# Reordering the last four experts of a fused attention, MLP and mixture-of-experts kernel, and the side work that is spread over two of its sections

## The chip, the cores and the metric

The kernel runs on one core of a Trainium2 chip. The metric is the device time of one execution, in microseconds (us). Several executions were timed; the median is the figure of merit, and one more execution was recorded by the hardware profiler. TensorE (PE) does the matmuls, VectorE (DVE) and ScalarE (ACT) the elementwise work, GpSimd (POOL) issues the indirect DMAs, and SyncE (SP) issues all other DMAs, each engine in its own program order.

## The reference

Three stages follow each other. The change touches only the last one, a mixture of eight experts on 2304 tokens:

```python
def _moe2_ref(x, w_skip, w_gate, w1, w2):
    do_compute = x @ w_skip > 0
    out = x.copy()
    xc = x[do_compute]
    logits = xc @ w_gate
    e_idx = np.argmax(logits, axis=1)
    ...
    for e in range(E):
        mask = e_idx == e
        h = np.maximum(xc[mask] @ w1[e], 0.0)
        y[mask] = gate_w[mask, None] * (h @ w2[e])
    out[do_compute] = xc + y
    return out
```

A token goes to one expert, or to none. `w1[e]` is 512 x 1024 and `w2[e]` is 1024 x 512, in float32. So an expert has eight pieces of 128 x 1024 numbers (512 KB each): pieces 0 to 3 are `w1`, pieces 4 to 7 are `w2`. The program calls the two groups of four the halves 0 and 1 of an expert: "2-1" is `w2` of expert 2, "3-0" is `w1` of expert 3.

## The kernel before

**How an expert is prepared.** All experts but one are multiplied in float16, each weight as the sum of a high and a low part. A half is loaded by four DMAs (`load_w`, in order on SP; "l" or "m" in the table below), its sums of squares or maxima are taken ("s", `stat_w`: ACT with `Square`, or DVE), a power of two is worked out from them ("c", `scale_w`, with one tiny matmul into a tile `ns`), and it is split ("p", `split_p`): per piece one ACT copy that writes the high part and one DVE instruction that writes the low part. Expert 3 (`PLAIN`) is multiplied in float32 and needs only its loads.

**How an expert is computed.** `block` takes 64 or 128 tokens. Its first half multiplies the gathered tokens by `w1` into tiles `hp`; ACT makes `r` and `hh` of them, DVE the low part of `hh`; its second half multiplies by `w2` into `y`; ACT scales that into `o`, and POOL adds the rows of `o` to the output by an indirect DMA. Below, 1f and 1s are the first and the second half of expert 1's block, 3f and 3s those of expert 3's, and so on.

**The order.** Experts 0, 6, 4 and 5 come first, each in sections of its own: a first section of 64 tokens, then a section of 128 behind a branch on the expert's count. Experts 1, 2, 3 and 7 (`LAST`) share one last section, one block each: 64 tokens for 1, 2 and 7, and 128 for 3. `GATHERS` says which gathers of tokens (expert, block) are issued in which section, by POOL, each with a transposing DMA on SP. `PREP` says which side work is done in which section: `5:` is expert 5, with its first and second section parted by `|`, and `8:` stands for the last section. Loads of a section that are marked "l" are issued at its start, those marked "m" later. Inside a section a planner (`Recorder.order`) sorts the instructions of each engine by assumed durations, so the program order of an engine is fixed when the kernel is built. When a section begins behind a branch, the semaphores of all engines are brought to common values, so an engine can wait for the end of another engine's preceding section.

Of the kernel before, what the change touches and what calls it, by code (L numbers as in the profile page):

```python
# [347 lines left out]
def tile_kernel(ctx, tc, q, k, v, w_in, w_out, w_skip, w_gate, w1, w2, out):  # L348
# [1163 lines left out]
    def prep_steps(e, which, wait=0.0):  # L1512
        P_ = functools.partial
        return ([("stat", P_(stat_w, e, which, x)) for x in range(4)] + [("scale", P_(scale_w, e, which, wait))]
                + [("split", P_(split_p, e, 4 * which + x)) for x in range(4)])
# [7 lines left out]
    def load_half(e, which, at=0.0):  # L1523
        for x in range(4):
            load_w(8 * e + 4 * which + x, at)
# [77 lines left out]
    def fac_w(e):  # L1603

        f = sm.tile([128, 1], F32, tag="fac", bufs=2, name="fac")
        fs = lst[:, e, :, 1]
        if e in PLAIN:
            return fs
        hs = half[:, e, C0[e], 1:2]
        rc.vector.tensor_tensor(out=f, in0=nrm[e][:, 0, 7:8], in1=nrm[e][:, 1, 7:8], op=ALU.mult)  # L1610
        rc.vector.tensor_scalar(out=fs, in0=fs, scalar1=f, scalar2=2.0 ** 20, op0=ALU.mult, op1=ALU.mult)
        if e in SMALL:
            rc.vector.tensor_scalar(out=hs, in0=hs, scalar1=f, scalar2=2.0 ** 20, op0=ALU.mult, op1=ALU.mult)
        return fs
# [77 lines left out]


    ORDER = [0, 6, 4, 5]
    LAST = [1, 2, 3, 7]
    XP = {0: 1, 6: 2, 4: 0, 5: 1}

    def place_of(e, j):
        if e in LAST:
            i = LAST.index(e)  # L1700
            h = (X2[2 - i // 2 * 2], i % 2) if j == 0 else (X2[1], 1) if j == 1 else (X2[3], j % 2)
        else:
            h = X2[XP[e] if j < 2 else 3], j % 2
        return h[0][:, :, 128 * h[1]:128 * h[1] + 128]

    def gather_to(e, j):
        gather(gix[:, e, C0[e] + j:C0[e] + j + 1], place_of(e, j))

    def pre_gather(e):
        for j in range(2):  # L1710
            gather_to(e, j)

    GATHERS = {0: [], 6: [(6, 2), (4, 0), (4, 1)], 4: [(4, 2), (5, 0), (5, 1), (1, 0), (2, 0)], 5: [(5, 2), (3, 0), (7, 0)]}

    PREP = {int(e): [x.split() for x in h.split("|")] for e, h in (y.split(":") for y in (
        "6:l1-1 m2-0 c5-0 p5-0 s1-0|c5-1 p5-1|s1-1,4:l2-1 m7-0 c1-0 p1-0|c1-1 p1-1 s2-0|s2-1,"
        "5:l7-1 m3-0 c2-0 p2-0|c2-1 p2-1,8:l3-1 s7-0 s7-1 c7-0 p7-0 c7-1 p7-1").split(","))}

    def aside_of(e, part):
        return PREP.get(e, [])[part:part + 1]  # L1720
# [6 lines left out]
    def split_beside(e, part):  # L1727
        for h in sum(aside_of(e, part), []):
            if h[0] == "m":
                load_half(int(h[1]), int(h[3]), 5.0)  # L1730
            if h[0] in "lm":
                continue
            for kind, f in prep_steps(int(h[1]), int(h[3]), 13.0 if e == 8 else 3.0):
                if kind[1] == {"s": "t", "c": "c", "p": "p"}[h[0]]:
                    rc.atom()
                    rc.shift = -150000 if kind == "scale" else 0
                    f()
                    if h[0] == "s":
                        rc.ready[len(rc.steps) - 1] = 4.0
                    rc.shift = 0  # L1740

    def tokens(e, j, xT, fs, par=None):

        c = C0[e] + j
        if j == 0 and e in SMALL:
            block(e, xT[:, :, 64:128], hix[:, e, c:c + 1], half[:, e, c, 1:2], j if par is None else par, 64)
        else:
            block(e, xT, six[:, e, c:c + 1], fs[:, c:c + 1], j if par is None else par)

    def first_tokens(e, fs):  # L1750

        rc.begin()
        rc.late = rc.left
        rc.urgent = True
        load_beside(e, 0)
        tokens(e, 0, place_of(e, 0), fs)
        rc.urgent = False
        for g in GATHERS[e]:
            gather_to(*g)
        split_beside(e, 0)  # L1760
        rc.issue()

    def last_tokens():

        rc.begin()
        rc.late = rc.left
        load_beside(8, 0)
        split_beside(8, 0)
        rc.urgent = True
        fs = {e: fac_w(e) for e in LAST}  # L1770
        for i, e in enumerate(LAST):
            tokens(e, 0, place_of(e, 0), fs[e], i)
        rc.urgent = False
        rc.issue()
        rc.left = {}
        with tc.If(cnt["last"] > 128, preferred_fallthrough_block=True, label="last"):
            for e in LAST:
                read_count(e)
                more_tokens(e, 1, fs[e])
# [5 lines left out]
    def more_tokens(e, j, fs):  # L1785
# [4 lines left out]
        with tc.If(cnt[e] > 128 * j, preferred_fallthrough_block=True, label=f"n{e}_{j}") as cmp:  # L1790
            if j < TM // 128:
                hint(e, j + 1, cnt[e])
                rc.begin()
                rc.late = rc.left if j else {}
                rc.urgent = True
                for x in ((1, 2, 3) if e in LAST or e == 0 else (3,)) if j == 1 else ():
                    gather_to(e, x)
                tokens(e, j, place_of(e, j), fs)
                rc.urgent = False
                if aside:  # L1800
                    split_beside(e, j)
                rc.issue()
                now = rc.left
                more_tokens(e, j + 1, fs)

            else:
                the_rest(e, fs)
# [76 lines left out]
    def read_count(e):  # L1884
        x = 16 if e == "last" else e
        cnt[e] = nc.values_load(ni[0:1, x:x + 1], min_val=0, max_val=NT)  # L1886
# [63 lines left out]
```

## Time and profile before

| what | us |
|---|---|
| median of 3 runs | 755.23 |
| lowest and highest of them | 749.65, 756.22 |
| profiled execution, its time | 757.81 |
| profiled execution, span from first to last instruction | 756.1 |
| PE busy in it | 688.2 |
| DVE, ACT busy | 582.8, 519.7 |

Times in the rows below are counted from the start of the span. The last section runs from 712.16 us to the end.

### The profile page before, as it was taken

The page shows a single profiled execution, that of the slowest core. Times are in us where ns is not written, and L with a number is a line of the kernel's source. Part 1 is how long each engine was busy: PE and PEld are TensorE (multiplying, and loading weights), DVE is VectorE, ACT ScalarE, POOL GpSimd, SP SyncE. Part 2 cuts the span into 40 slices and gives each one's busy share as a digit, 9 for nine tenths or more (in the row PEclk, how much of TensorE's full clock was granted, in tenths as well). Part 3 has the DMA queues.
Part 4 walks back from the last instruction along what each step waited for, and adds up shares of the span by engine and source line. Part 5 has one row for each costly group of instructions (what it writes and reads, how often), then busy time and mean ns, then how long its engine had stood idle before and what let it go on. Part 6 is the DMA issues. An engine that isn't in the chain of part 4 may idle for free. (4 is left out here: it accounts for less than half of the span.)

```text
span 756.1 us, 17807 instructions
## 1 busy us (share of the span) xinstructions
PE 688.2 (91%) x6696; PEld 471.3 (62%) x6696; DVE 582.8 (77%) x1688; ACT 519.7 (69%) x1100; POOL 84.1 (11%) x122
## 2 busy tenths in 40 slices
PE   4769987899999999988999999999999999997894
PEld 3548633586467666646656666757576677675683
DVE  5987997788899998978859965899778655554662
ACT  5876555799998886877748844767366558584681
POOL 2000000001000100000100010010105033243311
PEclk9999998899999999999999999999999999999998
DMA  9899999887597999879937537927065775989951
GB/s 256 239 236 316 269 251 202 188 150 134 111 192 146 162 190 197 163 131 194 161 53 165 101 63 177 386 67 225 33 196 147 212 169 122 231 195 238 292 145 16
DMA packets 280859, 134.52 MB, mean 178 GB/s; under 512 B 250347, under 2 KB 259061, under 8 KB 280240
## 3 DMA queue, kind: packets, MB, share of 16 engines
q1 hardware_dynamic: 276560, 125.68, 73.4%
q0 software_dynamic: 4192, 7.49, 4.7%
q8 instruction: 57, 0.93, 0.5%
q14 instruction: 50, 0.41, 0.2%
HBM read 74.38 MB, written 12.75 MB: 115 GB/s over the span
## 5 line engine op out<-in xcount | busy, mean ns | idle before, releaser
L310 PE MATMUL h<-xt,win 128*128 128x256 f16 x1344 | 158.4, 273 | 1.5 <-DVE n L310 1.0
L310 PE MATMUL y<-wout,g 128*128 128x512 f16 x672 | 157.0, 381 | 0.0
L310 PEld LDWEIGHTS <-win 128*128 128x128 f16 x1344 | 128.7, 98 | 22.7 <-DVE n L310 1.1
L310 PEld LDWEIGHTS <-g 128*128 128x128 f16 x672 | 64.3, 98 | 67.8 <-issue 2.0
L310 ACT ACTIVATE e<-s,mx 128x512 f32<-128x512 f32 (+4 forms) x160 | 81.9, 514 | 29.7 <-DVE ehl L310 13.5
L310 ACT ACTIVATE ehl<-e,su 128x512 f16<-128x512 f32 (+4 forms) x160 | 80.0, 548 | 15.1 <-DVE su L310 9.5
L310 DVE SCALAR_TENSOR_TENSOR ehl<-e,su,ehl 128x512 f16<-128x512 f32 (+4 forms) x160 | 81.4, 536 | 7.8 <-ACT ehl L310 7.5
L310 DVE TENSOR_REDUCE mx<-s 128x1 f32<-128x512 f32 (+4 forms) x160 | 74.8, 474 | 15.6 <-PE s L310 15.3
L310 PE MATMUL s<-kt,qt 128*128 128x384 f16 (+5 forms) x384 | 71.3, 311 | 11.9 <-ACT e L310 10.1
L310 PE MATMUL h<-xt,twi 128*128 128x256 f32 x256 | 64.0, 406 | 1.4 <-ACT xt L310 1.4
L310 PE MATMUL y<-two,g 128*128 128x512 f32 x128 | 62.6, 626 | 0.5 <-DVE two L310 0.5
L310 PEld LDWEIGHTS <-vt 128*64 128x64 f16 x1440 | 41.4, 115 | 32.4 <-issue 26.6
L310 PE MATMUL xps<-et,vt 128*64 128x128 f16 (+1 forms) x1440 | 50.7, 220 | 11.0 <-DMA et<-ehl 6.4
L310 PEld LDWEIGHTS h<-xt,twi 128*128 128x128 f32 x256 | 50.8, 204 | 9.6 <-ACT xt L310 2.1
L310 PEld LDWEIGHTS <-p 128*128 128x128 f16 x984 | 47.0, 99 | 14.0 <-issue 6.9
L310 ACT ACTIVATE el<-h,col 128x512 f32<-128x512 f32 x56 | 38.2, 682 | 24.7 <-PE h L310 24.3
L310 ACT ACTIVATE g<-el,col 128x512 f16<-128x512 f32 x56 | 40.1, 716 | 13.5 <-DVE el L310 12.8
L310 PEld LDWEIGHTS <-qt 128*128 128x128 f16 (+1 forms) x384 | 28.8, 106 | 28.5 <-issue 13.3
L1509 DVE SCALAR_TENSOR_TENSOR p<-p,n,p 128x1024 f16<-128x1024 f32 x32 | 40.7, 1278 | 4.7 <-ACT p L1508 4.5
L310 DVE SCALAR_TENSOR_TENSOR g<-el,col,g 128x512 f16<-128x512 f32 x56 | 41.6, 742 | 2.4 <-ACT g L310 2.3
L310 DVE SCALAR_TENSOR_TENSOR el<-h,col,el 128x512 f32<-128x512 f32 x56 | 41.6, 744 | 1.6 <-DVE el L310 0.5
L310 POOL DMA_INDIRECT lst_d<-li,si x16 | 18.0, 1126 | 201.5 <-DVE li L310 100.4
(233 smaller groups left out, 1166.3 us busy)
## 6 DMA issues: line engine op xcount, KB each, us to landing
p<-in_moe_w_dram SPq DMA_DIRECT2D x49, 512.0 KB
rw<-in_moe_w_in_dram SPq DMA_DIRECT2D x16, 512.0 KB
rw<-in_moe_w_out_dram SPq DMA_DIRECT2D x16, 512.0 KB
pb<-in_moe_w_dram SPq DMA_DIRECT2D x10, 512.0 KB
vflat<-in_v_dram SPq DMA_DIRECT2D x4, 1152.0 KB
out_dram<-pay SPq DMA_DIRECT2D x18, 256.0 KB
pay_d<-pay SPq DMA_DIRECT2D x18, 256.0 KB
raw<-in_k_dram SPq DMA_DIRECT2D x16, 256.0 KB
```

The costliest lines, as they stand in the source:

```text
L310: rec.call(e, time, lambda: getattr(self.real, op)(*args, **kw), reads, writes, dma)
L1509: rc.call("dve", 1.2, lambda: nc.vector.scalar_tensor_tensor(out=half(1), in0=raw.t, scalar=sc, in1=half(0), op0=ALU.mult, op1=ALU.subtrac ...
```

## The change

Three tables and one condition are edited, and nothing else.

```diff
-    LAST = [1, 2, 3, 7]
+    LAST = [1, 3, 2, 7]
...
-    GATHERS = {0: [], 6: [(6, 2), (4, 0), (4, 1)], 4: [(4, 2), (5, 0), (5, 1), (1, 0), (2, 0)], 5: [(5, 2), (3, 0), (7, 0)]}
+    GATHERS = {0: [], 6: [(6, 2), (4, 0), (4, 1)], 4: [(4, 2), (5, 0), (5, 1), (1, 0), (3, 0)], 5: [(5, 2), (2, 0), (7, 0)]}
...
         "6:l1-1 m2-0 c5-0 p5-0 s1-0|c5-1 p5-1|s1-1,4:l2-1 m7-0 c1-0 p1-0|c1-1 p1-1 s2-0|s2-1,"
-        "5:l7-1 m3-0 c2-0 p2-0|c2-1 p2-1,8:l3-1 s7-0 s7-1 c7-0 p7-0 c7-1 p7-1").split(","))}
+        "5:l7-1 m3-0 c2-0 p2-0|s7-0,8:l3-1 c2-1 p2-1 s7-1 c7-0 p7-0 c7-1 p7-1").split(","))}
...
-            for kind, f in prep_steps(int(h[1]), int(h[3]), 13.0 if e == 8 else 3.0):
+            for kind, f in prep_steps(int(h[1]), int(h[3]), 13.0 if e == 8 and h[1] == "7" else 3.0):
```

The last number tells the planner the earliest time, in us from the section's start, that it is to assume for the tiny matmul of a scale.

On ACT, in the second section of expert 5 (`n7` and `jk` belong to the sums of expert 7, `n2` to the split of expert 2, `o2` is the output of the block). The piece of the difference begins behind one more sum of `p1`, which now stands some rows earlier:

```order
 L310 ACTIVATE hh_12044<-r32_12043 128x256
-L1508 ACTIVATE p20_7248<-pb5_1495,n2_87 128x1024
-L1508 ACTIVATE p21_7249<-pb6_1496,n2_87 128x1024
+L1476 ACTIVATE jk_7251,n7_92<-p2_7230 128x1024
+L1476 ACTIVATE jk_7251,n7_92<-p3_7231 128x1024
+L1476 ACTIVATE jk_7251,n7_92<-p4_7232 128x1024
 L310 ACTIVATE o2_1511<-y2_12032,lists_1501 128x512
-L1508 ACTIVATE pb5_1495<-p23_1477,n2_87 128x1024
-L1508 ACTIVATE pb6_1496<-p0_7228,n2_87 128x1024
```

The four split copies of half 2-1 have left, two of them from behind `o2`; four sums of half 7-0 have come, all ahead of `o2`, which is now the last ACT instruction of the section.

On PE, in the last section, where 1f ends (`pd0` is the last piece of 1-0). Before, 2f follows, with the pieces of 2-0 (`p12`, `p13`, ...):

```order
L310 LDWEIGHTS pd0_1498
L310 MATMUL hp_12738<-mxwo2_1509,pd0_1498 128x64
L310 LDWEIGHTS p12_7240
L310 MATMUL hp_12742<-mxwo2_1509,p12_7240 128x64
...
L310 LDWEIGHTS p13_7241
```

Now 3f follows, with the pieces of 3-0 (`p8` to `p11`), then a scale's tiny matmul and 1s (`y2_12706`):

```order
L310 MATMUL hp_12710<-mxwo2_1509,pd0_1498 128x64
L310 MATMUL hp_12715<-x32_12713,p8_7236 128x128
L310 MATMUL hp_12715<-x32_12713,p9_7237 128x128
L310 MATMUL hp_12715<-x32_12713,p10_7238 128x128
L310 MATMUL hp_12715<-x32_12713,p11_7239 128x128
...
L310 MATMUL ns_12697<-cb_12696,ones16_75 128x1
L310 LDWEIGHTS hh_12709
L310 MATMUL y2_12706<-pd1_1499,hh_12709 64x256
```

The whole row of halves on PE was 1f, 2f, 1s, 2s, 3f, 3s, 7f, 7s. It is now 1f, a quarter of 3f, 1s, the rest of 3f, 3s, 2f, 7f, 2s, 7s. On SP nothing moves: the loads of 3-0 and 3-1 stand where they stood, and two of the four of 3-1 go to other buffers. On POOL two of the four last output adds change places.

## Rows read from the trace of the kernel before

**Rows 1.** PE's timeline, last section: start, duration, engine, line, operation, count, idle before.

```profile
712.16 0.48 PE L310 MATMUL hp<-mxwo,p 128*128 128x64 f16 x6 [2.89 <-ACTq L1790]
...
716.20 1.86 PE L310 MATMUL hp<-mxwo,p 128*128 128x64 f16 x58
718.41 1.27 PE L310 MATMUL hp<-mxwo,p 128*128 128x64 f16 x38 [0.36 <-issue]
719.61 1.50 PE L310 MATMUL y<-pd,hh 128*64 128x256 f16 x24
...
722.25 1.48 PE L310 MATMUL y<-p,hh 128*64 128x256 f16 x24
...
724.97 2.05 PE L310 MATMUL hp<-x,p 128*128 128x128 f32 x16
...
732.44 7.03 PE L310 MATMUL y<-p,r 128*128 128x512 f32 x16
739.31 0.25 PE L310 MATMUL hp<-mxt,p 128*128 128x64 f16 x3
...
744.23 1.48 PE L310 MATMUL y<-p,hh 128*64 128x256 f16 x24
```

**Rows 2.** POOL's timeline, the last output add.

```profile
746.50 1.55 POOL L1682 DMA_INDIRECT out_dram<-o,gp  x1 [4.27 <-ACT o L310]
```

**Rows 3.** ACT's timeline, second section of expert 5 and one sum of expert 7.

```profile
706.25 2.19 ACT L1508 ACTIVATE p<-pb,n 128x1024 f16<-128x1024 f32 x2 [0.74 <-DVE n L310]
709.30 0.69 ACT L310 ACTIVATE o<-y,lists 128x512 f32<-128x512 f32 x1 [0.86 <-PE y L310]
709.89 2.17 ACT L1508 ACTIVATE pb<-p,n 128x1024 f16<-128x1024 f32 x2
...
717.34 1.04 ACT L1476 ACTIVATE jk<-p 128x1024 bf16<-128x1024 f32 x1
718.29 0.19 ACT L1476 ACTIVATION_READ_ACCUMULATOR jk<-p 128x1 f32 x1
```

**Rows 4.** Timeline at an earlier branch, the start of expert 5's first section.

```profile
688.01 0.69 ACT L310 ACTIVATE o<-y,lists 128x512 f32<-128x512 f32 x1 [2.46 <-PE y L310]
...
688.94 0.42 PE L310 MATMUL hp<-mxt,p 128*128 128x64 f16 x9 [0.97 <-ACTq L1790]
```

**Rows 5.** Windows: busy time and count of each engine, granted clock, DMA share, GB/s.

```profile
712.10:715.00 2.90, 2.84 (x55) 2.84 (x55) 1.67 (x4) 0.03 (x1) 1.65 (x1) 0.51 1.00 404
```

**Rows 6.** SP's timeline: transposes of gathers, loads of 3-0, a transpose, loads of 3-1.

```profile
706.36 3.27 SPq L310 DMA_TRANSPOSE mxt<-gp  x2
709.69 2.00 SPq L1458 DMA_DIRECT2D p<-in_moe_w_dram  x4
719.33 2.10 SPq L310 DMA_TRANSPOSE mxwo<-gp  x1
722.39 1.94 SPq L1461 DMA_DIRECT2D p<-in_moe_w_dram  x4
```

**Rows 7.** DMA queues (packets, MB, share): 711.7:714; 714:716; 716:718; 718:719.3, two queues; 719.3:719.8.

```profile
q1 hardware_dynamic: 214, 0.81, 87.3%
...
q1 hardware_dynamic: 221, 0.78, 97.7%
...
q1 hardware_dynamic: 75, 0.30, 40.4%
...
q0 software_dynamic: 104, 0.20, 82.8%
q1 hardware_dynamic: 48, 0.14, 28.8%
...
q1 hardware_dynamic: 2, 0.00, 0.6%
```

**Rows 8.** DMA queue q1 in 730.3:731.6, the end of the loads of 3-1.

```profile
q1 hardware_dynamic: 10, 0.02, 3.7%
```

**Rows 9.** DVE's timeline, low parts of two pieces of expert 7.

```profile
735.94 2.47 DVE L1509 SCALAR_TENSOR_TENSOR pb<-p,n,pb 128x1024 f16<-128x1024 f32 x2
```

## The prediction, made before the changed kernel was run

> **What bounds the kernel now.** I read the page first: PE is busy for 688.2 of 756.1 us, so what counts is where PE waits. The change leaves everything alone up to expert 5's second section, so I went to PE's timeline of the last section, and from each wait to the engine that ends it.
>
> PE comes to the last section with its longest wait of this stretch, 2.89 us, ended by ACT at the branch, and starts at 712.16 [rows 1]. ACT's timeline shows what it was: behind the block's output `o`, which is ready at 709.30 + 0.69 = 709.99, stand two more split copies of half 2-1, which end at 712.06 [rows 3]. From there PE has no wait longer than 0.36 us. Its last matmuls end at 744.23 + 1.48 = 745.71 [rows 1], the last output add follows at 746.50 [rows 2], and some 10.4 us of tail go to the end of the span. So the section is 33.55 us of PE, and the end of the kernel is the end of PE plus a constant.
>
> Two parts of the 33.55 us aren't work. The granted clock stood at 0.51 in the first 2.9 us after the wait [rows 5], that is at 1.2 instead of 2.4 GHz. What it cost is seen by two equal halves: 1f took 716.20 - 712.16 = 4.04, 2f 1.86 + 1.27 = 3.13, so 0.91 us. The idle of 0.36 inside 2f is the other. The work itself is 33.55 - 0.91 - 0.36 = 32.28 us. By parts: each of 1f, 2f, 7f 3.13; 1s 722.25 - 719.61 = 2.64, 2s 2.7, 7s about 2.8; 3f 732.44 - 724.97 = 7.47; 3s 739.31 - 732.44 = 6.87 [rows 1].
>
> **Part 1: the side work of expert 5's second section.** Four ACT copies (2.19 / 2 = 1.1 us each) and four DVE low parts (2.47 / 2 = 1.24) of half 2-1 leave, with their scale; four sums of 7-0 come, 1.04 to 1.2 us each with the read of the accumulator [rows 3, 9]. One sum stands before the block's third `r`, three stand between the last `hh` and `o`. The three need some 3.5 us, and ACT was free of the block's work from 706.25 - 0.74 = 705.5 to 709.30, so `o` stays at 709.3, give or take 0.2. Then it is ACT's last instruction there. At the branch before expert 5's first section, where `o` was the last too, PE began at 688.94, 0.24 us behind the end of `o` at 688.70, with an idle of 0.97 [rows 4]. So PE should restart at 709.99 + 0.24 = 710.23, 1.93 us earlier. With the shorter idle it should keep the full clock: there the first nine matmuls took 0.42 [rows 4], here the first six 0.48 [rows 1]. 1f then ends at 710.23 + 3.13 = 713.36 instead of 716.20: 2.84 us are won at this point.
>
> **Part 2: expert 3 moves ahead of expert 2.** PE goes on with 3f now, not with 2f. Half 3-0 is loaded by four DMAs, and SP issues them only at 709.69 to 711.69, behind the transposes of the gathers [rows 6]; the change moves nothing on SP, and what those transposes wait for lies ahead of the edited section. When do the four pieces land? No row of before shows a wait for them, since 3f began at 724.97. The DMA queues do. From 711.7 on queue q1 carries only these loads, 4 x 0.524 = 2.10 MB: 0.81 MB go in 711.7 to 714, 0.78 until 716, 0.30 until 718 and 0.14 until 719.3, and two packets after that [rows 7]. In the slow end queue q0 takes 82.8% of the engines against 28.8% for q1; that is the gather of a further block of expert 5 and the output add, which stay where they are. So the fourth piece is complete between 719.3 and 719.8; I take 719.7. Each result tile of 3f needs all four pieces in turn, and the fourth matmul of the block stands in PE's program order ahead of everything else.
>
> So PE does three float32 matmuls (3 of 32 in 7.47 us: 0.70) as pieces come in, and waits: 719.7 - 713.36 - 0.70 = 5.6 us of idle in all. Before, 2f filled that time. Queued behind the waiting matmul are the tiny matmul for 2-1's scale, so DVE's scale and ACT's copies of 2-1, and 1s; on ACT the `r` of 3f stands ahead of a sum of 7-1 and of these copies. None of that is due soon: 2s is the last but one half now.
>
> After 719.7 there remain 32.28 - 3.13 - 0.70 = 28.45 us of work: 748.15. A wait of that length, interrupted by single matmuls, will bring the low clock as the idle of 2.89 us did; I charge the same 0.91 us (bounds 0, and twice that for two such stretches): 749.06. Against 745.71 that is 3.35 us later.
>
> **Part 3: the rest, taken at nothing.** The gathers of 2 and 3 change places with equal sizes in the same slots of POOL and SP. The last section gets four copies (4.4 us on ACT) and four low parts (5.0 us on DVE) of 2-1 and loses four sums (4.4 us or more on ACT): for ACT nothing, for DVE 5 us, which lie beside PE's 32 us as long as none is due early (the third rival). Half 3-1 is issued at 722.39 and only 0.02 MB of it move in 730.3 to 731.6 [rows 6, 8]; 3s would start at 719.7 + 0.91 + 5 x 0.23 + 2.64 + 24 x 0.23 = 729.9, and needs the fourth piece three quarters of 6.87 later, at 735: no wait. The output adds of 2 and 7 follow each other by some 2.7 us at the end; one takes POOL 1.55 [rows 2], so the last isn't held up on POOL. Whether its landing is drawn out by the one before it no row shows: 0 to 1 us, I take 0.
>
> **The sum.** Won 1.93 + 0.91 + 0.36 = 3.20; lost 5.6 us of idle and 0.91 of clock: 3.3 us slower. The profiled execution would go from 757.81 to 761.1; it lies 2.6 above the median of the three runs, so for the median 755.23 + 3.35 = 758.6.
>
> **A page beside this.** The Trainium skill, "DMA: Bandwidth & Descriptors", section "Anatomy of one DMA — SWDGE (gpsimd) path", gives a DMA as about 2.0 us plus its bytes over 436 GB/s. As an estimate by that page 2.10 MB would be there 6.8 us after the first issue, at 716.5, and the changed kernel would come to 755.4. The trace disagrees: [rows 7] show the loads still moving 9.6 us after the issue. Its section "Queues, rings and completion order" says that a DMA engine takes turns between the queues, packet by packet; [rows 7] agree, where q1's share falls as q0's rises.
>
> **Rivals.**
> - *The wait is not there, and the change does what it seems made for.* 3-0 would have to be complete by 713.36 + 0.70 = 714.1. Then PE would reach 3s at 710.23 + 3.13 + 2.64 + 7.47 = 723.5, and now the loads of 3-1, issued at 722.39, would be late: their last packets are in 730.3 to 731.6 [rows 8]. The last quarter of 3s (1.72) and 2f, 7f, 2s, 7s (11.8) after that give 743.8 to 745.1, so 753.3 to 754.6, say 754: faster, by 0.2%. Against it: at 714 less than half of 3-0 had moved.
> - *The loads end sooner, since the gather stays out of their way.* At the rate of 711.7 to 716 (1.59 MB in 4.3 us) the rest would be there at about 717.3; the end is 2.4 us before the forecast's: 756.2. For it: one execution is all that is shown of these transfers. Against: the gather is issued by POOL on the end of a transpose that the change does not touch.
> - *A second wait, at 7f.* The scale of 7-0 and 7-1 hangs on two tiny matmuls that stand inside 3s now, a quarter and a half way through. DVE takes the result of the second before the first low part of 7-0: 3.4 us into 3s. Four low parts at 1.24 [rows 9] and some 1.1 us of small steps make 9.5, and 7f begins 6.87 + 3.13 = 10.0 us after the start of 3s. The margin is 0.5 us; from there each us that DVE or ACT is late counts in full, and a wait brings back the low clock. At 1.5 us late that is 1.5 + 0.9: 761.0.
> - *Part 1 does not do what it says* and PE restarts no sooner. Then 1f ends at 716.2 at the latest, still ahead of 719.0, and the forecast is unchanged: the time won by part 1 is spent waiting for 3-0 in any case.
>
> **Chances and range.** Forecast 0.68 (with the fourth rival in it), no wait 0.07, loads sooner 0.10, second wait 0.15. The forecast's own bounds: the landing as early after its issue as 3-1's earliest, 730.3 - 722.39 = 7.9 us, gives 2.1 less, 756.5; the clock at 0 gives 757.7, at twice the charge 759.5; a drawn-out last add 1 us more. With the second wait and the spread of the runs shown (749.65 to 756.22 for one kernel) the range is 754 to 762; it leaves out half of the first rival and the far end of the third. A time over 1% away (about what a measurement of this kernel can tell from no change) lies below 747.7 or above 762.8: 0.02 for faster; 0.08 for slower, if the second wait is 4 us or comes with two stretches of low clock; 0.90 between.
>
> **What would show it.** Right: in the changed profile the idle before the last section is about 1 us and 1f runs at full clock; the first float32 matmuls of 3f have idle of over 5 us before them, ended by a DMA of weights, to about 719.7; the granted clock falls behind that; PE ends near 749 and no half later on waits over 0.5 us. Wrong: 3f runs through (the loads came sooner, or PE came later than I say), PE still idles for 2.9 us at the branch (ACT is not what it waited for), or 7f waits for a low part.

## The result, and the profile of the changed kernel

The changed kernel took 759.73 us (median of 20 runs, 753.79 to 768.43), the kernel before in the same session 752.99 us (20 runs, 749.11 to 759.81). The ratio is 1.0072, with a 95% interval of 1.0050 to 1.0094; like all ratios here it leaves disturbed runs out, so it can differ from the ratio of the medians, which lie 6.74 us apart. By the ratio the change costs 0.7%, some 5.4 us (3.8 to 7.1). The profiled execution took 761.69 us, its span is 759.9 us.

TensorE's timeline of the last section answers to [rows 1]: start, duration, engine, line, operation, tile sizes, type and count, and in brackets the idle time ahead and what ended it.

```profile
701.25 5.55 PE L310 MATMUL y<-pb,hh 128*128 128x512 f16 x24
707.69 0.33 PE L310 MATMUL hp<-mxwo,p 128*128 128x64 f16 x6 [0.89 <-ACTq L1790]
...
710.40 0.25 PE L310 MATMUL hp<-mxwo,pd 128*128 128x64 f16 x3
712.11 0.46 PE L310 MATMUL hp<-x,p 128*128 128x128 f32 x2 [1.47 <-DVE hh L310]
714.50 0.80 PE L310 MATMUL hp<-x,p 128*128 128x128 f32 x2 [1.93 <-DMA p<-in_moe_w_dram]
716.89 0.79 PE L310 MATMUL hp<-x,p 128*128 128x128 f32 x2 [1.60 <-DMA p<-in_moe_w_dram]
719.52 2.50 PE L310 MATMUL hp<-x,p 128*128 128x128 f32 x10 [1.84 <-DMA p<-in_moe_w_dram]
721.82 0.21 PE L310 MATMUL ns<-cb,ones 128*128 128x1 bf16 x1
721.96 2.77 PE L310 MATMUL y<-pd,hh 128*64 128x256 f16 x24
724.52 1.57 PE L310 MATMUL y<-pc,hh 128*64 128x256 f16 x24
726.02 5.62 PE L310 MATMUL hp<-x,p 128*128 128x128 f32 x48
731.48 1.88 PE L310 MATMUL y<-p,r 128*128 128x512 f32 x4
...
738.57 2.96 PE L310 MATMUL hp<-mxt,p 128*128 128x64 f16 x96
741.37 2.96 PE L310 MATMUL hp<-mxt,pb 128*128 128x64 f16 x96
...
746.91 2.79 PE L310 MATMUL y<-p,hh 128*64 128x256 f16 x48
```

The idle at the branch has shrunk from 2.89 to 0.89, and 1f runs in 2.96 us (707.69 to 710.65) against 4.04. Then come four waits, 6.84 us in all, one for each piece of 3-0, with two rows of matmuls between each (a float32 matmul stands in the trace as two rows). The profile puts the first wait down to DVE's low part `hh`, which ended 0.14 us ahead of the matmul. It was the load all the same: the first piece landed 4.0 us after its issue, at 712.0, and in the run below where 3-0 is loaded earlier, with the same row on TensorE, that matmul starts at 707.13, ahead of the same `hh` (708.19 to 708.62). From 719.52 on TensorE doesn't idle; its last matmuls end at 749.70.

ACT's timeline of the changed kernel answers to [rows 3].

```profile
705.76 1.06 ACT L1476 ACTIVATE jk<-p 128x1024 bf16<-128x1024 f32 x1
706.73 0.19 ACT L1476 ACTIVATION_READ_ACCUMULATOR jk<-p 128x1 f32 x1
706.84 0.69 ACT L310 ACTIVATE o<-y,lists 128x512 f32<-128x512 f32 x1
...
722.06 0.38 ACT L310 ACTIVATE r<-hp 128x256 f32<-128x256 f32 x1 [9.51 <-PE ns L310]
```

SP's timeline of the changed kernel answers to [rows 6].

```profile
704.16 3.78 SPq L310 DMA_TRANSPOSE mxt<-gp  x2
707.99 2.01 SPq L1458 DMA_DIRECT2D p<-in_moe_w_dram  x4
717.07 1.28 SPq L310 DMA_TRANSPOSE mxwo<-gp  x1
719.30 1.94 SPq L1461 DMA_DIRECT2D p<-in_moe_w_dram  x4
```

`o` is now ACT's last instruction of the section and ends at 707.53; TensorE starts 0.16 us later. The loads of 3-0 are issued at 707.99, 0.30 us behind that start. ACT shows what queues behind the wait: an `r` that idles 9.51 us, with the copies of 2-1 behind it.

Windows of the changed kernel answer to [rows 5]; the last three columns are the granted clock, the DMA share and GB/s. The first is the wait's first part, the second the stretch of low clock (1.2 GHz), the third the rest of the section.

```profile
711.00:714.40 3.40, 0.46 (x2) 0.30 (x2) 0.42 (x1) 1.52 (x4) 1.09 (x1) 1.00 1.00 348
714.50:724.70 10.20, 6.76 (x41) 5.61 (x43) 2.31 (x9) 2.64 (x5) 0.00 (x0) 0.50 0.94 268
...
724.70:749.70 25.00, 25.00 (x380) 20.36 (x375) 19.12 (x32) 16.67 (x25) 5.53 (x3) 1.00 0.15 37
```

The low clock begins in the middle of the waits, lasts through them and for 5.2 us of work behind the last one. Before, it lasted 3.4 us.

The DMA queues in 714:716 and 716:718, which answer to the second and third window of [rows 7]:

```profile
q0 software_dynamic: 54, 0.18, 45.0%
q1 hardware_dynamic: 80, 0.29, 36.7%
...
q0 software_dynamic: 120, 0.23, 61.7%
q1 hardware_dynamic: 107, 0.36, 46.7%
```

The loads are issued 1.7 us earlier now, so these windows lie 6.0 to 10.0 us behind the first issue, where q1 was slow before too (0.30 MB in 716:718, 6.3 to 8.3 us behind). What is slower than before is the stretch from 4 to 6 us behind the issue: q1 moves 0.66 MB in it instead of 0.81, while q0 sets in sooner (0.08 MB against 0.02). The fourth piece is there at 719.5 (the wait's end), 11.5 us after the first issue, against 10.0 before.

### The profile page after: what moved, and what is told of

It is laid out like the page before. It is cut to its first block, busy times and chain, and to the rows that moved or that the text cites. A ratio compares the mean times of both kernels' runs of the same rounds, so it can differ in the third digit from the quotient of the medians.

```text
span 759.9 us, 17799 instructions
## 1 busy us (share of the span) xinstructions
PE 687.9 (91%) x6696; PEld 471.6 (62%) x6696; DVE 583.2 (77%) x1688; ACT 520.0 (68%) x1100; POOL 84.7 (11%) x122
## 5 line engine op out<-in xcount | busy, mean ns | idle before, releaser
L310 ACT ACTIVATE el<-h,col 128x512 f32<-128x512 f32 x56 | 38.3, 683 | 25.5 <-PE h L310 24.8
L310 PEld LDWEIGHTS <-p 128*128 128x128 f16 x960 | 44.8, 98 | 8.3 <-PEq L1790 4.1
L310 PEld LDWEIGHTS <-qt 128*128 128x128 f16 (+1 forms) x384 | 28.7, 105 | 30.2 <-issue 14.8
L310 PEld LDWEIGHTS <-hh 128*64 128x64 f16 (+1 forms) x432 | 29.5, 110 | 20.4 <-DVE hh L310 2.5
```

The source lines that it names most:

```text
L310: rec.call(e, time, lambda: getattr(self.real, op)(*args, **kw), reads, writes, dma)
```

## The experiments

All ratios are to the kernel before, measured in the same session. Where an experiment's profile is compared with another's, times are counted from the start of expert 5's first section on TensorE (688.94 in the trace before, 687.76 after), since that start itself lies anywhere from 682.9 to 690.4 in the traces. By that count TensorE ended at 56.8 before and at 61.9 after.

**Is it the order, or the side work?** Two runs take back one part each. The first, *order back*:

```diff
-    LAST = [1, 3, 2, 7]
+    LAST = [1, 2, 3, 7]
...
-    GATHERS = {... 4: [(4, 2), (5, 0), (5, 1), (1, 0), (3, 0)], 5: [(5, 2), (2, 0), (7, 0)]}
+    GATHERS = {... 4: [(4, 2), (5, 0), (5, 1), (1, 0), (2, 0)], 5: [(5, 2), (3, 0), (7, 0)]}
```

> The changed kernel with the order 1, 2, 3, 7 and the old gathers put back; the side work stays as changed. Late loads (PE waits at 3f for half 3-0, and pays low clock behind it): 2f and 1s fill the time until 3-0 is there, the shorter idle at the branch is kept, so PE has no wait over 1 us for a weight DMA in the first 12 us of the last section; 2 to 3 us faster than before (ratio 0.996 to 0.998), some 7 us faster than the changed kernel. Side work (moving the split of 2-1 into the last section costs the time): as slow as the changed kernel, ratio 1.005 to 1.008.

It took 756.32 us, ratio 1.0018 (0.9984 to 1.0052): no gain, a miss of the 0.996 to 0.998, though less than the 1.005 to 1.008 that the side work was to cost. Its timeline of TensorE shows why:

```profile
705.79 0.34 PE L310 MATMUL hp<-mxwo,p 128*128 128x64 f16 x6 [0.89 <-ACTq L1790]
...
717.95 0.80 PE L310 MATMUL hp<-x,p 128*128 128x128 f32 x2 [2.76 <-DMA p<-in_moe_w_dram]
719.53 2.50 PE L310 MATMUL hp<-x,p 128*128 128x128 f32 x10 [0.79 <-DMA p<-in_moe_w_dram]
```

The early restart is there, but the planner still put the first quarter of 3f ahead of the end of expert 2's work, and TensorE waited 3.55 us for 3-0 all the same. The list `LAST` doesn't fix the order of halves.

The second, *side work back*, has the old `PREP` and condition, and keeps the new order:

```diff
-        "5:l7-1 m3-0 c2-0 p2-0|s7-0,8:l3-1 c2-1 p2-1 s7-1 c7-0 p7-0 c7-1 p7-1").split(","))}
+        "5:l7-1 m3-0 c2-0 p2-0|c2-1 p2-1,8:l3-1 s7-0 s7-1 c7-0 p7-0 c7-1 p7-1").split(","))}
...
-            for kind, f in prep_steps(int(h[1]), int(h[3]), 13.0 if e == 8 and h[1] == "7" else 3.0):
+            for kind, f in prep_steps(int(h[1]), int(h[3]), 13.0 if e == 8 else 3.0):
```

> The changed kernel with the side work of before put back (2-1 split in expert 5's second section, sums of 7-0 in the last one); order 1, 3, 2, 7 and its gathers stay. Late loads: PE restarts some 2 us later behind the branch, but still ahead of the landing of 3-0, so the end is the same as in the changed kernel within 1 us, less the low clock that a shorter wait may save: ratio to before 1.004 to 1.008. Side work: as fast as before or within 0.2% of it.

It took 753.66 us, ratio 0.998 (0.9939 to 1.0020), a miss too: taken alone it is what was expected if the side work cost the time. But more than the side work had moved, as the planner now put 1s ahead of 3f:

```profile
709.12 0.34 PE L310 MATMUL hp<-mxwo,p 128*128 128x64 f16 x6 [2.90 <-ACTq L1790]
...
715.80 1.48 PE L310 MATMUL y<-pc,hh 128*64 128x256 f16 x24
717.21 2.05 PE L310 MATMUL hp<-x,p 128*128 128x128 f32 x16
```

With the late restart and 1s ahead, 3f began at 717.21, just behind the last piece of 3-0, and had no wait. So neither run takes back one part with the rest held. Over the three kernels the time went with the wait for 3-0: 6.84 us of it gave 1.0072, 3.55 gave 1.0018, none 0.998 (the last two are within each other's intervals). That the side work is not the cause is shown by the next run, which keeps it.

**Is the wait the loads' lateness?** The loads of 3-0 and 7-1 change places on SP, so that 3-0 is issued one section earlier:

```diff
-        "5:l7-1 m3-0 c2-0 p2-0|s7-0,...
+        "5:l3-0 m7-1 c2-0 p2-0|s7-0,...
```

> The changed kernel with the loads of 3-0 and 7-1 exchanged: 3-0 is issued at the start of expert 5's first section, 7-1 where 3-0 was. Late loads: no wait of PE for 3-0, full clock through 1f, 3f, 1s; 3s then comes to the loads of 3-1, issued late, and waits up to 2 us; 4 to 7 us faster than the changed kernel, ratio to before 0.997 to 1.001. If the low clock or the wait has another cause than the landing of 3-0: ratio stays 1.005 to 1.009.

It took 751.97 us, ratio 0.996 (0.9926 to 0.9993): 1.1% less than the changed kernel, faster than the kernel before, and a little better than expected. The new order and the new side work are both in it, so what cost the time in the changed kernel was that 3-0 came late for the new order. 3f, with 1s within it, ran through from 707.13 to 717.46. One wait was left, for 3-1, whose loads stand on SP behind a transpose:

```profile
704.04 0.33 PE L310 MATMUL hp<-mxwo,p 128*128 128x64 f16 x6 [0.89 <-ACTq L1790]
...
707.13 2.03 PE L310 MATMUL hp<-x,p 128*128 128x128 f32 x16
...
720.45 3.36 PE L310 MATMUL y<-p,r 128*128 128x512 f32 x4 [2.99 <-DMA p<-in_moe_w_dram]
```

The same exchange in the kernel before, *before, 3-0 early*:

> The kernel before, with the loads of 3-0 and 7-1 exchanged and nothing else: TensorE's row and ACT's stay word for word. Theory (the early load is of use only where expert 3 comes early): nothing in the kernel before waits for 3-0, so the time stays, ratio 0.998 to 1.002, and the gain of the changed kernel with this exchange (0.996) is one of order and load together. Rival (the exchange is a gain by itself, as it spreads the transfers better or lets 7-1's sums come at a better time): 0.994 to 0.997.

754.26 us, ratio 0.9986 (0.9954 to 1.0018), as the theory had it: where nothing waits for 3-0, its early load gives nothing that can be measured. The interval does not rule out a gain of 0.4%, so how much of the 0.996 is owed to the order and the load together stays open. And the exchange with the order back, *order back, 3-0 early* (both diffs together):

> The changed kernel with the loads of 3-0 and 7-1 exchanged, and with the order 1, 2, 3, 7 and the old gathers: the new side work and the early load are kept, expert 3 stands behind expert 2 again where the planner lets it. Theory (the early release of ACT is worth some 2 us, and expert 3's place matters only as long as it is waited for): no wait for 3-0, and the wait for 3-1 that the kernel with the exchange alone had (2.99 us at 3s) shrinks, since 3s comes later: ratio 0.993 to 0.997, the same as with expert 3 ahead or 1 to 2 us less. Rival (the place ahead of 2 is a gain once the load is early, since it gives 2-1's split more time): 0.998 to 1.002.

753.21 us, ratio 0.997 (0.9944 to 0.9996), no wait for a DMA in the last section. This is the slow end of what was expected, and the rival's 0.998 to 1.002 is not ruled out; with the load early, expert 3 ahead of expert 2 or (but for a quarter of 3f, which the planner put ahead of 2s) behind 2f is the same within the interval.

**Is the gather what makes the loads late?** The gather of expert 5's further block and its transpose are moved behind the branch to that block, which this input does not take:

```diff
-                for x in ((1, 2, 3) if e in LAST or e == 0 else (3,)) if j == 1 else ():
+                for x in ((1, 2, 3) if e in LAST or e == 0 else (3,)) if j == 1 and e != 5 else (3,) if j == 2 and e == 5 else ():
```

> The changed kernel without the gather of expert 5's fourth block in its second section (it moves behind a branch that these inputs do not take). If that gather draws out the landing of 3-0 (it shares the DMA engines): the last piece of 3-0 is there 1.5 to 3 us earlier after its issue (7.5 to 9 us instead of 10 to 11.5), and 3-1 is issued right behind 3-0: 2 to 4 us faster than the changed kernel, ratio to before 1.001 to 1.004. If the landing is set by the queue alone: 10 us or more after the issue as before, ratio 1.006 to 1.008.

758.38 us (749.96 to 769.34), ratio 0.9986 (0.9946 to 1.0026): the medians give 1.0041, so over so wide a spread the time stays unclear. The trace is plainer. The loads of 3-1 followed 4.1 us behind the first of 3-0 instead of 11.3, but POOL, freed of the gather, issued the output add of expert 5 at 704.42, ahead of the loads instead of behind them, and the wait for the first piece grew:

```profile
712.00 0.77 PE L310 MATMUL hp<-x,p 128*128 128x128 f32 x2 [4.71 <-DMA p<-in_moe_w_dram]
713.25 0.80 PE L310 MATMUL hp<-x,p 128*128 128x128 f32 x2 [0.48 <-DMA p<-in_moe_w_dram]
714.73 0.80 PE L310 MATMUL hp<-x,p 128*128 128x128 f32 x2 [0.69 <-DMA p<-in_moe_w_dram]
716.03 2.29 PE L310 MATMUL hp<-x,p 128*128 128x128 f32 x9 [0.50 <-DMA p<-in_moe_w_dram]
```

The sum, 6.38 us, is hardly less than 6.84, in part as the loads came 1.21 us behind TensorE's restart and not 0.30. The fourth piece was there 10.5 us after the first issue (11.5 in the trace after), where 7.5 to 9 were expected if the gather drew it out: with all that follows from its move the gather gives no more than 1 us, and it alone is not the cause. With the early load as well, *3-0 early, gather off*:

> The kernel with the loads of 3-0 and 7-1 exchanged, which had one wait of 2.99 us left, for the loads of 3-1 (issued behind a transpose that waits for a gather of a further block of expert 5, of which this input has none); here that gather and its transpose are moved behind the branch to that further block. No computation is left out: the gather is issued only when its block is computed. Theory: 3-1 is issued some 6 us sooner, the wait at 3s is gone and with it its low clock of 3.4 us: 3 to 4.5 us less than without the gather's move, a ratio of 0.990 to 0.994. Rival (the transfers share the engines' time, and the output add that now comes ahead of the loads takes what the gather took): the wait shrinks by less than 1 us, 0.995 to 0.997.

753.79 us, ratio 0.9965 (0.9934 to 0.9995). The wait at 3s is gone from its trace, yet the time is that of the exchange alone and that of the rival, so the expected further gain is a miss. The trace can't settle why: in this execution TensorE idled 3.43 us in expert 5's first section ("issue", at 689.77), and came to the last section 6 us later than in the run without the gather's move. So late it might have met hardly any wait with the gather in place.

**What does the low clock cost?** Useless matmuls fill the wait:

```diff
...
                     if e in PLAIN:
+                        for _ in range((6, 8, 7, 7)[kk] if ff == 0 and fill else 0):
+                            rc.call("pe", 0.0, lambda: nc.tensor.matmul(out=ys[0], lhsT=xT[:, 0, :], rhs=xT[:, 0:4, :], start=True, stop=True), [xT], [])
...
```

> The changed kernel with 28 float16 matmuls of 128 x 512 (6, 8, 7 and 7) put into TensorE's row ahead of the first four float32 matmuls of expert 3, just where it waits for the four pieces; their result is never read, and every other row of every engine stays as it is. At full clock one takes 0.21 us (24 of 128 x 512 took 5.55 in the changed kernel's trace at 701.25, some of them overlapping weight loads), so 28 take 6.0 to 6.5 of the 6.84 us of idle. Theory (a part of the loss is the low clock that the wait brings, 10.24 us of it in the trace after, of which 6.5 us of work behind the wait would have taken 3.9): the clock stays full behind the wait, and the kernel gains about 2.6 us on the changed one: a ratio of 1.003 to 1.005 to the kernel before, and 726.0 - 719.5 = 6.5 us from the end of the wait to the second group of float32 matmuls shrinks to about 4. Rival (the loss is the wait alone, the slow stretch being work that the DMAs hold up in any case): the ratio stays at 1.006 to 1.009. If the filler outlasts the landing by some 0.5 us, both are that much later.

761.75 us, ratio 1.0070 (1.0039 to 1.0100), where a gain was expected: a miss. The time tells nothing on the clock, since in the profiled execution there was no wait to fill: TensorE reached the last section at 708.50, 5.4 us behind the first issue of 3-0, so the filler (6, 8, 7 and 7 matmuls from 713.24 on) stood in its way for some 6 us. But the clock stayed full, and so this trace has the price of the work behind the wait:

```profile
719.95 1.28 PE L310 MATMUL hp<-x,p 128*128 128x128 f32 x10
721.06 0.17 PE L310 MATMUL ns<-cb,ones 128*128 128x1 bf16 x1
721.16 1.50 PE L310 MATMUL y<-pd,hh 128*64 128x256 f16 x24
722.49 1.48 PE L310 MATMUL y<-pc,hh 128*64 128x256 f16 x24
723.90 5.62 PE L310 MATMUL hp<-x,p 128*128 128x128 f32 x48
```

From the fourth piece's matmul to the next float32 group it is 723.90 - 719.95 = 3.95 us here and 726.02 - 719.52 = 6.50 after; from there to the end of TensorE both take 23.68. So the low clock cost 2.55 us behind the wait.

**Does the earlier restart matter?** Three useless ACT copies (1.95 us) stand behind `o`, and every other instruction stays where it was:

```diff
...
         rc.scalar.activation(out=o, in_=ys[0][:, 0:512 // m], func=AF.Copy, scale=fc)
+        for _ in range(3 if late else 0):
+            rc.steps[-1][5].append(lambda: nc.scalar.activation(out=junk.t[:, 0:512], in_=o, func=AF.Copy))
...
```

> The changed kernel with three useless ACT copies of 128 x 512 (0.69 us each by the trace, 2.1 in all) behind the output copy o of expert 5's second section; every other row of every engine stays, so now the earlier release of ACT (part 1 of the change) is taken back alone, with TensorE's order held. Theory (the fourth rival of the prediction: the time that part 1 wins at the branch is spent waiting for 3-0): TensorE restarts about 2 us later against the loads' issue, the idle ahead of 3f shrinks by as much, and the time stays: ratio 1.005 to 1.009. Rival (the restart sets the end): 2.1 us slower than the changed kernel, 1.009 to 1.012.

757.77 us, ratio 1.0040 (1.0008 to 1.0073): a little below the 1.005 to 1.009 of the theory, which the interval reaches, so not slower than the changed kernel, and the rival's 1.009 to 1.012 is outside. The waits shrank by the time that the copies took and more:

```profile
705.46 0.34 PE L310 MATMUL hp<-mxwo,p 128*128 128x64 f16 x6 [3.51 <-ACTq L1792]
...
713.06 0.80 PE L310 MATMUL hp<-x,p 128*128 128x128 f32 x2 [0.82 <-DMA p<-in_moe_w_dram]
715.59 1.65 PE L310 MATMUL hp<-x,p 128*128 128x128 f32 x6 [1.74 <-DMA p<-in_moe_w_dram]
```

TensorE ended at 745.65, 30.06 us behind the matmul of the fourth piece; after, it was 749.70 - 719.52 = 30.18. So the end went with the landing of 3-0, not with the restart.

**How steady is the wait?** The changed kernel was profiled twice more and the kernel before once more.

> The changed kernel once more, unaltered, to see another execution's profile: in two of the experiments TensorE came to the last section some 5 us later against the start of expert 5 than in the trace after, by idle that the profile puts down to issue. Theory: where it comes early the four pieces of 3-0 are waited for, 5 to 7 us in all with a stretch of low clock behind; where it comes late the wait shrinks by as much, and the end against the last piece's landing stays at 30.2 us or less. Rival: the wait is of the same size whenever TensorE comes.

> As the run before: a third execution of the changed kernel, with the same two expectations.

> The kernel before once more, unaltered, for the same comparison: the idle at the branch of the last section is again 2.9 to 3.0 us, ended by ACT, with 3.4 us of low clock behind it, and no wait for a DMA in the last section; from the start of the last section to the end of TensorE some 33.5 us.

The changed kernel took 761.45 and 757.97 us. The four waits of the first of them, all put down to loads (as in the second):

```profile
712.62 0.46 PE L310 MATMUL hp<-x,p 128*128 128x128 f32 x2 [1.95 <-DMA p<-in_moe_w_dram]
713.79 0.49 PE L310 MATMUL hp<-x,p 128*128 128x128 f32 x2 [0.71 <-DMA p<-in_moe_w_dram]
716.96 0.79 PE L310 MATMUL hp<-x,p 128*128 128x128 f32 x2 [2.67 <-DMA p<-in_moe_w_dram]
719.07 1.22 PE L310 MATMUL hp<-x,p 128*128 128x128 f32 x4 [1.32 <-DMA p<-in_moe_w_dram]
```

They make 6.65 us, in the second 5.80; the low clock lasted 10.24 us in both, and the end came 30.47 and 30.76 us behind the fourth piece's matmul, where 30.2 or less was expected. TensorE's restart lay 20.3 and 21.1 us behind the start of expert 5 (19.9 in the trace after), so neither was one of the late ones. That the wait shrinks with a late restart rests on the run with the ACT copies, and on that with the filler, where TensorE restarted at 24.8 by the same count and had no wait. The kernel before took 759.87 us, with 2.89 us of idle at the branch and no wait for a DMA behind it, as expected. Two things were not: the last section took 34.60 us, as TensorE idled 1.97 us ("issue") within 2f, and no low clock followed the idle at the branch.

## Why the prediction was right in direction and short in size

The forecast was 3.35 us slower, a ratio of 1.0044, and 5.4 us or 1.0072 were measured, with an interval that begins at 1.0050. Every step of the mechanism is in the trace, and two terms of the sum were too small. That TensorE went on at 719.52, close to the 719.7 of the forecast, is chance: it had come to the branch 2.5 us sooner than forecast and then waited longer.

- **The restart.** The end of ACT's last instruction was to be followed by TensorE 0.24 us later; it was 0.16 (0.16 and 0.09 in the further executions). Measured that way the gain is 2.17 - 0.16 = 2.01 us for a forecast of 1.93, and 1f kept the full clock.
- **The wait at 3f.** It came where it was put, ended by the loads, and all four pieces were waited for. It was 6.84 us (6.65 and 5.80 in the further executions) and not 5.6. The landing of the fourth piece was read from one execution as 10.0 us after the first issue. It was 11.5, 11.3 and 10.8 in three executions of the changed kernel. In the second execution of the kernel before it was some 11.7, as an estimate: the last packet of 3-0 ended 11.1 us after the first issue there, and in the trace after TensorE's matmul follows the last packet by 0.6 us. So the term was mis-sized by the spread of the transfers, of which the first trace before happened to show the low end; the bounds of the prediction reached below it (7.9) and not above. A further 0.8 us came from SP issuing the loads 0.30 us behind the restart instead of 0.54 ahead of it; this varies too (1.36 behind and 0.28 ahead in the further executions).
- **The low clock.** The step "I charge the same 0.91 us" was the other short term: 2.55 us. The idle before was one stretch of 2.89 us and the low clock lasted 3.4; here four stretches with single matmuls between them gave 10.24, part of it spent waiting, at no cost, the rest on work. The bound "twice that" was still below. The work itself behind the landing was 27.63 us and not 28.45, mainly as 2f and 7f took 2.8 to 2.9 us each in place of 3.13. So from the landing on the sum is 30.18 against 29.36.
- **The sum.** From the restart to the end of TensorE it is 42.01 us after and 33.55 before: 8.46 more, less the 2.01 of the earlier restart, 6.45 by the traces. Forecast: 3.35. Of the 3.1 between them 2.36 is the landing against the restart and 0.82 the work and clock behind it, less 0.08 of the restart. The 5.4 us of the timed runs lie between; their 3.8 to 7.1 hold the 6.45 and not the 3.35.
- **The rivals.** No wait: it did not come about in any trace of the changed kernel. Loads sooner: the gather came sooner too, issued 0.67 us behind the first load instead of 1.12, and without it the wait was hardly less. Second wait at 7f: the margin of 0.5 us was 0.25 and held; DVE's last of the four low parts that 7f needs ends at 738.65 + 2.47 = 741.12, and the matmuls begin at 741.37 without idle:

```profile
738.65 2.47 DVE L1509 SCALAR_TENSOR_TENSOR pb<-p,n,pb 128x1024 f16<-128x1024 f32 x2
```

- **The fourth rival's statement**, that the time won by part 1 is spent waiting, was shown by the ACT copies: TensorE restarted 2.6 us later behind the start of expert 5 (22.6 against 19.9), and the end stayed 30.1 us behind the landing. The run with the old side work could not show it, since the planner sorted TensorE's row anew.
- **The page beside it.** The Trainium skill, "DMA: Bandwidth & Descriptors", section "Anatomy of one DMA — SWDGE (gpsimd) path", states its 2.0 us plus bytes over 436 GB/s for one DMA that GpSimd issues. The estimate worked out from it for the four loads that SP issues, 6.8 us from the first issue, was too low: the traces of the two kernels have 10.0 to 11.7 us, with transposes and gathers beside the loads.

What stays open: in the runs with the early load, what further gain the gather's move would bring, and what makes TensorE come to the last section up to 6 us later in some executions. A part of it the traces show: with the filler an idle of 2.53 us ("issue") in expert 5's first section was followed by 10.24 us of low clock, and with the early load and the gather off 3.43 us by 6.83.

## What to carry to other kernels

An engine released earlier gains nothing if the next thing in its row is a load whose issue stays where it was: move the load with the work that needs it. Here the change alone cost 0.7%, and with one exchange in the row of loads it gained 0.4%, while that exchange alone did nothing that can be told from no change. When a landing time carries the sum, take its spread from several transfers, not the one value that a profile shows; and when one part of a planned kernel is taken back for a test, compare the rows of the engines first, as the planner may move the rest.

## What was not expected of the hardware

The low clock lasted 10.24 us in all three executions of the changed kernel, and 3.41 us behind a single wait of 2.89 or 2.99 us; behind two waits of 2.76 and 0.79 us, with the order back, it lasted 6.83 us; with the ACT copies, where an idle of 3.51 us at the branch was followed by two waits, it lasted 13.65 us from 706.88 on. An idle of 2.89 us at the branch in the second execution of the kernel before was followed by none. TensorE also idles, by "issue", for 0.5 to 2 us within 1f or 2f in some executions and not in others of the same kernel (1.97 us at 719.80 in the kernel before, none above 0.36 in its first trace), which with the transfers makes the last section differ by 1 or 2 us without any edit. Of the 16 idles by "issue" of 0.9 us or more that all traces have from expert 5 on, 15 end 1.2 to 1.6 us after a 16 KB packet of queue q8, which the profile calls "instruction": in the first trace before the packet ended at 690.60 and TensorE went on at 691.99; in the trace of the changed kernel the two are 688.77 and 690.01. In the run with the early load that packet ended at 685.13, ahead of TensorE's start at 685.20, and there was no such idle in expert 5's first section. That would fit a wait for the next part of the program, but no run tests it.
